# A fused attention and feed-forward kernel: the order of the first batch's loads and products

## The chip, the cores and the metric

The kernel runs on one core of one Trainium2 chip. The metric is the time of one execution on the device in microseconds (us). An execution with the hardware profiler on gives the span, from the first to the last instruction of the program, and the trace that the lines below come from.

## The reference

Attention without softmax over 8 batches of 12 heads, 448 positions and 64 values a head, then a gated feed-forward layer over the 3584 rows that come out:

```python
scores = (1.0 / np.sqrt(64)) * np.matmul(q, k.transpose(0, 1, 3, 2))
attn = np.maximum(scores, 0.0) ** 2 / 448
x = np.matmul(attn, v).transpose(0, 2, 1, 3).reshape(3584, 768)
gate = np.maximum(x @ w_gate, 0.0)      # w_gate, w_val: 768 x 1536
val = x @ w_val
out = (gate * val) @ w_out              # w_out: 1536 x 768
```

Inputs and output are float32. Products are made in bfloat16.

## The kernel before

**Loads.** GpSimd (POOL) issues all loads (`dma_in`, L246), and they turn float32 into bfloat16 on the way. They run on one queue in the order of the calls at the end of the kernel (L689 to L724), and POOL holds eight of them outstanding: each issue waits for the load eight places ahead of it. `load_heads(b, h0, n, what)` loads keys and queries (tile `qk`, two DMAs) or values (tile `vv`, two DMAs) of n heads. `load_gv(c)` loads 256 columns of `w_gate` and of `w_val` (tiles `wg`, `wv`, 384 KB each), `load_out(c)` half the columns of `w_out` (tiles `wo`).

**Attention.** Three groups g of four heads per batch. Batches 0 and 1 transpose `qk` on TensorE (PE) against an identity (`transpose_pair`, L346, tile `t_ps`) and copy the result to `qkT` (L355). Batches 2 to 7 are transposed by DMA: VectorE (DVE) gathers the rows into `spare` (seven copies, L377), then SyncE (SP) issues two DMA transposes (L387), which write `qkT`. A copy of one element, `mark` (L712), on POOL waits for them ahead of the next batch's loads. Scores come in steps `Part.s(i)`: the product (L469, and L475 for the last 64 keys, the tail), relu on ScalarE (ACT, L485) or DVE (L487), square on DVE (L503, tile `at` or `spare`). `Part.pv` multiplies by the values (L525, L531) and a copy (L547, L549) fills `xT`.

**Batch 0 in two parts.** Its queries are cut into a part A of 192 columns and a part B of 256, so that the feed-forward of part A can begin early. The order of batch 0's PE work is a string, `ORDER` (L754): `T2` is a transpose step of two heads, `A1:0` score step 0 of group 1 in part A, `VA1` that group's product with values, `W2` two products of 128x512 on zeros whose result is not used (`idle`, L334); an `f` has the step use two single banks of PSUM, and `/` begins a new burst. Eight products on zeros run ahead of all (`first_zeros`, L747).

**Feed-forward.** For each block of 128 columns mf, a gate product (`g_ps`) and a value product (`v_ps`), six matmuls each (L578), then relu (L585, L587) and the product of both on DVE (L592) into `hT`. Each waits for its `xT` and its weight block. In batch 0 the order over parts and blocks is made by `ffn_ops` (L606): part A with the first `n1` blocks, part B with the same, then both in turn. Output tiles follow: per 128 rows two products of 12 matmuls (L630, `o_ps`), copies on ACT (L643), and two stores of 64 rows on SP (L674). Over two batches there are seven such tiles.

**Order on the engines.** `plan` (L103) walks through the attention list, the feed-forward list, the loads and the rest with rough costs, and so fixes the order in which each engine's instructions stand. Between attention bursts of later batches it puts feed-forward work worth `gap`, which is the work left in the batch divided by the bursts left (L158 to L160). On the chip each engine takes its own instructions in that order.

Of the kernel before, what the change touches and what calls it, by code (L numbers as in the profile page):

```python
# [102 lines left out]
def plan(att, ffn, others, pool, nburst, calm):  # L103

    P = Planner()
    ai = fi = pi = 0
    pend = list(others)
    last_burst = None  # L110
    since = 0.0
    gap = 0.0
    while ai < len(att) or fi < len(ffn) or pend or pi < len(pool):
        cands = []
        for op in pend:
            b = P.best(op)
            if b is not None:
                cands.append((b[0], op.prio, b[2], 1, b[1], op))
        if pi < len(pool):
            b = P.best(pool[pi])  # L120
            if b is not None:
                s = b[0]
                if pi >= P.NOUT:
                    s = max(s, P.landed[pi - P.NOUT])
                cands.append((s, 0, 0.0, 0, "POOL", pool[pi]))
        A = P.best(att[ai][0]) if ai < len(att) else None
        F = P.best(ffn[fi][1]) if fi < len(ffn) else None
        pick = None
        if A is not None and F is not None:
            if att[ai][1] == last_burst:  # L130
                pick = "A" if A[0] <= F[0] + 0.3 else "F"
            elif since >= gap:
                pick = "A" if A[0] <= F[0] + 0.1 else "F"
            else:
                pick = "F" if F[0] <= A[0] + 0.1 else "A"
        elif A is not None:
            pick = "A"
        elif F is not None:
            pick = "F"
        if pick == "A":  # L140
            cands.append((A[0], 2, A[2], 2, "PE", att[ai][0]))
        elif pick == "F":
            cands.append((F[0], 2, F[2], 2, "PE", ffn[fi][1]))
        assert cands, "no operation can start"
        s, _, _, kind, e, op = min(cands, key=lambda c: c[:4])
        P.commit(op, s, e)
        if kind == 0:
            pi += 1
        elif kind == 1:
            pend.remove(op)  # L150
        elif pick == "A":
            if att[ai][1] != last_burst:
                last_burst = att[ai][1]
                since = 0.0
            ai += 1

            b0 = ffn[fi][0] if fi < len(ffn) else None
            work = sum(o.engs["PE"] for b, o in ffn[fi:fi + 60] if b == b0)  # L158
            left = nburst(b0, last_burst) if b0 is not None else 1
            gap = work / max(1, left) if left > 0 and last_burst >= calm else 0.0  # L160
        else:
            since += op.engs["PE"]
            fi += 1
    order = sorted(range(len(P.ops)), key=lambda i: (P.ops[i].start, i))
    return [P.ops[i] for i in order]
# [3 lines left out]
def kernel(  # L169
# [14 lines left out]
    B, H, S, D = q.shape  # L184
# [5 lines left out]
    NT = S // P2  # L190
    NC = NT // 2
# [5 lines left out]
    KF = d_ff // 128  # L197
# [47 lines left out]
    def dma_in(dst, src, n_desc, kb, deps=(), alloc=(), rate=380.0):  # L245
        op = Op({"POOL": 0.58 + 0.0004 * n_desc}, lambda: nc.gpsimd.dma_start(out=dst(), in_=src),  # L246
                deps=deps, alloc=alloc, xfer=kb / rate)
        op.lat = 0.75 if n_desc <= 128 else 1.3
        pool_ops.append(op)
        return op  # L250

    wg_op, wv_op, wo_op = {}, {}, {}

    def load_gv(c):
        cols = slice(c * WC, (c + 1) * WC)
        wg = moe_w_gate.rearrange("(kd p) f -> p kd f", p=128)
        wv = moe_w_val.rearrange("(kd p) f -> p kd f", p=128)
        wg_op[c] = dma_in(lambda: w_gate_sb[c], wg[:, :, cols], 768, 720)
        wv_op[c] = dma_in(lambda: w_val_sb[c], wv[:, :, cols], 768, 720)

    def load_out(c):
        wo = moe_w_out.rearrange("(kf p) m -> p kf m", p=128)
# [17 lines left out]
    def load_heads(b, h0, n, what="kv"):  # L280
        if b not in bat:
            bat[b] = Batch()
            bat[b].buf = Buf(r_in, NT if b >= XBAR_FROM else HP)
            bat[b].vbuf = Buf(r_v, NQ * len(PARTS(b)))
            bat[b].tbuf = Buf(r_xb, NQ * (2 * NC + 1) if b > 0 else NQ * (NC + 1) * len(PARTS(b)))
            bat[b].qk_op, bat[b].v_op = {}, {}
        st = bat[b]

        def tile_of(name, n):
            if not hasattr(st, name):  # L290
                setattr(st, name, inp.tile([128, H, n, D], BF16, name=name))
            return getattr(st, name)

        hs = slice(h0, h0 + n)
        rows = lambda x: x[b, hs].rearrange("h (p t) d -> p h t d", t=NT)
        rate = (240.0 if h0 == 4 else 290.0) if b == 0 else 340.0
        if "k" in what:
            k_op = dma_in(lambda: tile_of("qk", NT)[64:128, hs], rows(k), 64 * n, 112 * n, rate=rate, alloc=[st.buf] if h0 == 0 else [])
            q_op = dma_in(lambda: tile_of("qk", NT)[0:64, hs], rows(q), 64 * n, 112 * n, rate=rate)
            for h in range(h0, h0 + n):  # L300
                st.qk_op[h] = (k_op, q_op)
        if "v" in what:
            v0 = dma_in(lambda: tile_of("vv", NC + 2)[0:64, hs, 1:NC + 2], rows(v)[:, :, 0:NC + 1], 64 * n, 64 * n,
                        alloc=[st.vbuf] if h0 == 0 else [], rate=340.0)
            v1 = dma_in(lambda: tile_of("vv", NC + 2)[64:128, hs, 0:NC + 1], rows(v)[:, :, NC:NT], 64 * n, 64 * n, rate=340.0)
            for h in range(h0, h0 + n):
                st.v_op[h] = (v0, v1)

# [27 lines left out]
    def transpose_pair(b, g, j):  # L336

        st = bat[b]
        ps = Buf(r_f, 1)
        box = {}  # L340

        def emit():
            t_ps = box["t"] = bank("t_ps", BF16)
            for i, t in enumerate(slot_order(b)):
                for h2 in range(2):
                    nc.tensor.transpose(t_ps[64 * h2:64 * h2 + 64, i * 128:(i + 1) * 128],  # L346
                                        st.qk[:, 4 * g + 2 * j + h2, t, :], ident)

        def emit_copy():
            dst = columns_of(b)[:, :, 2 * g + j, :].rearrange("p a (t c) -> p t a c", c=P2)  # L350
            src = box["t"][:, :2 * S].rearrange("p (t a c) -> p t a c", t=NT, a=2)
            if cp.eng == "ACT":
                nc.scalar.copy(dst, src)
            else:
                nc.vector.tensor_copy(dst, src)  # L355

        h = 4 * g + 2 * j
        op = Op({"PE": 0.5 if g or b else 0.95}, emit, deps=list(st.qk_op[h]) + list(st.qk_op[h + 1]) + [id_op],
                alloc=[ps], reads=[st.buf])
        cp = Op({"DVE": 0.57, "ACT": 0.84}, emit_copy, deps=[op], alloc=[st.tbuf] if g == 0 and j == 0 else [],  # L360
                reads=[ps], prio=0, bias=0.0)
        others.append(cp)
        t_op[(b, 2 * g + j)] = cp
        return op
# [199 lines left out]
    def gv_ops(b, c0, n, mf):  # L564
# [28 lines left out]

        pe = {"PE": 0.03 + 6 * n / 2400.0}
        ga, va, gs = Buf(r_f, 1), Buf(r_f, 1), Buf(r_g, 1)
        gop = Op(pe, lambda: product("g_ps", w_gate_sb), deps=xop[(b, c0)] + [wg_op[c]], alloc=[ga], reads=[st.x_buf])
        grel = Op(on_psum(n), None, deps=[gop], alloc=[gs], reads=[ga], prio=0)
        grel.emit = lambda: emit_relu(grel)
        vop = Op(pe, lambda: product("v_ps", w_val_sb), deps=xop[(b, c0)] + [wv_op[c]], alloc=[va], reads=[st.x_buf])
        vmul = Op({"DVE": 0.09 + n / 960.0}, emit_mul, deps=[vop, grel], alloc=[hs["buf"]] if first else [],  # L600
                  reads=[va, gs], prio=0)
        hs["mul"].append(vmul)
# [3 lines left out]
    def ffn_ops(b):  # L606
        res = []
        if len(PARTS(b)) == 2:
            pa, pb = PARTS(b)
            n1 = KF // 2  # L610
            order = [(pa, m) for m in range(n1)] + [(pb, m) for m in range(n1)]
            order += [(p, m) for m in range(n1, KF) for p in (pa, pb)]
        else:
            order = [(PARTS(b)[0], m) for m in range(KF)]
# [76 lines left out]
    id_op = Op({"POOL": 0.35}, identity)  # L691
    pool_ops.append(id_op)
    load_heads(0, 4, 4, "k")
    load_heads(0, 0, 4, "v")
    load_heads(0, 8, 4, "k")
    load_heads(0, 4, 8, "v")
    load_gv(0)
    load_gv(1)
    load_gv(2)
    load_heads(1, 0, 4)  # L700
    load_gv(3)
    load_heads(1, 4, 4)
    load_gv(4)
    load_gv(5)
    load_out(0)
    load_heads(1, 8, 4)
# [40 lines left out]
    def first_zeros():  # L747
# [3 lines left out]
    att.append((Op({"PE": 3.0}, first_zeros), nb))  # L751


    ORDER = ("T0 W2 T1 A0:0f A0:1 W2 A0:3 W2 A0:2 T2 T3 A1:0 A1:1f A1:3 T4 T5 A1:2 A2:0 A2:1f A2:2 VA0f A2:3 "  # L754
             "B0:0 VA1f B0:3 VA2f B0:1f B0:2 / B1:0 B2:0 VB0f / / B2:1f / B1:2 B2:3 B1:3 B1:1 / / B2:2 VB1f VB2")
    for x in ORDER.split():
        part = {"A": A, "B": Bp}
        single = x[-1] == "f"
# [78 lines left out]
```

## Time and profile before

| | |
|---|---|
| runs | 437.32, 438.71, 438.66, 439.34 us; median 438.69 |
| profiled execution | 437.32 us, span 435.6 us |
| mean granted clock of TensorE | 0.995 |
| PE busy | 424.9 us (98%) in 3014 matmuls |
| DVE, ACT, POOL busy | 231.5, 198.6, 46.3 us |
| first products: gate and value (L578), outputs (L630) | 127.3, 127.0, 113.2 us |
| HBM read, written | 48.76 MB, 11.01 MB |

The engines run side by side; each waits for another only through semaphores. In a timeline row stand the start, the time taken (of several instructions in a row, marked x), the engine, the line, the operation with out<-in, the shape, and in brackets the idle time before it with what ended it. A `POOL` row of a load or an `SPq` row of a store is its issue; the data land later. PEclk is the share of TensorE's clock that was granted.

### The profile page before, as it was taken

What the parts mean: (1) busy time and instruction counts of PE and PEld (TensorE: products, weight loads), DVE (VectorE), ACT (ScalarE), POOL (GpSimd) and SP (SyncE); (2) the same over time, 40 slices, a digit from 0 to 9 for tenths busy, and PEclk for the clock granted to TensorE, in tenths of its full rate; (3) what the DMA queues carried; (4) which work ended last, traced back from release to release, by engine and by line L of the source; (5) the groups of instructions that cost most, each with busy time, mean ns of one, the idle gap of its engine ahead of it and who ended that gap; (6) DMA issues with size and microseconds to landing.
All of it is one profiled execution on the core that took longest, in us unless ns stands there. A gap on an engine that the chain in (4) does not pass through costs nothing.

```text
span 435.6 us, 7425 instructions
## 1 busy us (share of the span) xinstructions
PE 424.9 (98%) x3014; PEld 223.7 (51%) x3014; DVE 231.5 (53%) x411; ACT 198.6 (46%) x340; POOL 46.3 (11%) x72
## 2 busy tenths in 40 slices
PE   6799999999999999999999999999999999999996
PEld 2577875444454444544455444554445444555553
DVE  3796776177625775674653746545643456202200
ACT  3685455345634554554454545544544444332221
POOL 8546210010001002000200200010000000000000
PEclk9899999999999999999999999999999999999999
DMA  8999999980289567927937990980003200040014
GB/s 111 195 198 198 202 201 214 141 147 14 40 160 203 71 87 106 208 55 109 169 67 118 166 151 15 150 146 2 0 2 86 62 0 2 9 101 0 2 36 108
DMA packets 75170, 44.12 MB, mean 101 GB/s; under 512 B 34560, under 2 KB 71680, under 8 KB 75136
## 3 DMA queue, kind: packets, MB, share of 16 engines
q0 software_dynamic: 37856, 24.38, 39.7%
q1 hardware_dynamic: 37200, 19.17, 22.8%
q8 instruction: 23, 0.38, 0.3%
q10 hardware_dynamic: 80, 0.10, 0.1%
q14 instruction: 11, 0.09, 0.1%
HBM read 48.76 MB, written 11.01 MB: 137 GB/s over the span
## 4 chain that ended last, share of the span: by engine, by line
PE 93%; DMA 4%; POOL 1%; ACT 1%; SPq 0%; issue 0%; DVE 0%; POOLq 0%
PE o_ps L630 26%; PE g_ps L578 25%; PE v_ps L578 25%; PE s_ps L469 7%; PE s_ps L531 6%; DMA qkT<-spare 2%; DMA qk<-in_q_dram 2%; PE s_ps L475 2%; PE s_ps L525 1%; POOL qk L246 1%; PE t_ps L346 1%; PE x_ps L531 1%; ACT r_sb L485 0%; POOL vv L246 0%; SPq L387 0%
## 5 line engine op out<-in xcount | busy, mean ns | idle before, releaser
L578 PE MATMUL g_ps<-xT,wg 128*128 128x448 bf16 (+2 forms) x648 | 127.3, 332 | 0.1
L578 PE MATMUL v_ps<-xT,wv 128*128 128x448 bf16 (+2 forms) x648 | 127.0, 332 | 0.0
L485 ACT ACTIVATE r_sb<-s_ps 128x896 bf16<-128x896 f32 (+4 forms) x146 | 99.8, 739 | 36.0 <-PE s_ps L469 25.1
L592 DVE TENSOR_TENSOR hT<-v_ps,g_sb 128x448 bf16<-128x448 f32 (+2 forms) x108 | 61.5, 569 | 102.0 <-PE v_ps L578 101.9
L630 PE MATMUL o_ps<-wo,hT 128*128 128x384 bf16 x672 | 113.2, 326 | 0.0
L503 DVE TENSOR_TENSOR at<-r_sb 128x896 bf16<-128x896 bf16 (+4 forms) x163 | 93.6, 612 | 22.3 <-ACT r_sb L485 22.1
L585 ACT ACTIVATE g_sb<-g_ps 128x448 bf16<-128x448 f32 (+2 forms) x106 | 53.9, 508 | 110.5 <-PE g_ps L578 107.8
L630 PEld LDWEIGHTS <-hT 128*128 128x128 bf16 x672 | 63.9, 98 | 48.7 <-issue 8.0
L487 DVE TENSOR_SCALAR r_sb<-s_ps 128x448 bf16<-128x448 f32 (+5 forms) x72 | 62.5, 898 | 49.7 <-PE s_ps L469 49.5
L578 PEld LDWEIGHTS <-wv 128*128 128x128 bf16 x648 | 61.0, 98 | 50.7 <-issue 5.8
L578 PEld LDWEIGHTS <-wg 128*128 128x128 bf16 x648 | 59.8, 98 | 52.7 <-issue 10.4
L643 ACT ACTIVATE o_sb<-o_ps 128x384 f32<-128x384 f32 (+1 forms) x56 | 27.4, 489 | 71.6 <-PE o_ps L630 71.6
L469 PE MATMUL s_ps<-qkT 64*128 64x448 bf16 (+2 forms) x324 | 37.5, 336 | 1.8 <-DVE qkT L355 1.1
L531 PE MATMUL s_ps<-at,vv 128*64 128x448 bf16 x252 | 27.8, 357 | 0.0
L547 ACT CAST xT<-s_ps 128x896 bf16<-128x896 f32 (+1 forms) x22 | 19.6, 892 | 12.7 <-PE s_ps L531 12.7
L469 PEld LDWEIGHTS <-qkT 64*128 64x128 bf16 x324 | 11.8, 95 | 22.5 <-issue 15.5
L531 PEld LDWEIGHTS <-vv 128*64 128x64 bf16 x324 | 15.6, 109 | 14.1 <-issue 7.0
L246 POOL DMA_DIRECT2D vv<-in_v_dram x22 | 15.5, 717 | 46.4 <-PE s_ps L531 36.0
L712 POOL COPY mark<-qkT 64x1 bf16<-64x1 bf16 x5 | 0.9, 182 | 173.2 <-DMA qkT<-spare 173.2
L377 DVE COPY spare<-qk 128x768 bf16<-128x768 bf16 x42 | 12.3, 351 | 0.7 <-DMA qk<-in_q_dram 0.7
L355 DVE COPY qkT<-t_ps 128x896 bf16<-128x896 bf16 x12 | 7.1, 621 | 9.4 <-PE t_ps L346 9.3
L346 PE MATMUL t_ps<-ident,qk 128*64 128x128 bf16 x168 | 6.7, 235 | 3.3 <-DMA qk<-in_q_dram 2.6
(31 smaller groups left out, 83.6 us busy)
## 6 DMA issues: line engine op xcount, KB each, us to landing
out_dram<-o_sb SPq DMA_DIRECT2D x54, 192.0 KB, 2.8
vv<-in_v_dram POOLq DMA_DIRECT2D x12, 384.0 KB, 12.4
qk<-in_k_dram POOLq DMA_DIRECT2D x6, 672.0 KB, 7.3
qk<-in_q_dram POOLq DMA_DIRECT2D x6, 672.0 KB, 10.0
wg<-in_moe_w_gate_dram POOLq DMA_DIRECT2D x6, 384.0 KB, 11.2
wv<-in_moe_w_val_dram POOLq DMA_DIRECT2D x6, 384.0 KB, 11.9
wo<-in_moe_w_out_dram POOLq DMA_DIRECT2D x2, 1152.0 KB, 19.2
qk<-in_k_dram POOLq DMA_DIRECT2D x5, 224.0 KB, 10.1
```

The source lines that it names most:

```text
L246: op = Op({"POOL": 0.58 + 0.0004 * n_desc}, lambda: nc.gpsimd.dma_start(out=dst(), in_=src), deps=deps, alloc=alloc, xfer=kb / rate)
L469: nc.tensor.matmul(half_of(h2)[:, m * n:(m + 1) * n], lhsT=kq(1, j, h2, key_off(b) + c * 128, 128), rhs=kq(0, j, h2, self.c0, n), start=Tr ...
L485: nc.scalar.activation(dst, src, AF.Relu)
L487: nc.vector.tensor_scalar_max(dst, src, 0.0)
L503: lambda: nc.vector.tensor_tensor(self.at_tile(i), loc["r"][:, :2 * ne], loc["r"][:, :2 * ne], ALU.mult),
L531: nc.tensor.matmul(x_of(o, j), lhsT=st.vv[:, 4 * g + 2 * j + h2, 1 + c, :], rhs=self.at(j, c, h2), start=False, stop=(c == NC - 1))
L547: nc.scalar.copy(dst, src)
L578: nc.tensor.matmul(ps, lhsT=w[c][:, kd, o:o + 128], rhs=st.xT[:, kd, cols], start=(kd == 0), stop=(kd == KD - 1))
L585: nc.scalar.activation(loc["gs"], loc["g_ps"], AF.Relu)
L592: nc.vector.tensor_tensor(hs["hT"][:, mf, t0:t0 + n], loc["v_ps"], loc["gs"], ALU.mult)
L630: nc.tensor.matmul(loc["o"], lhsT=hs["hT"][:, kf, ti * 128:(ti + 1) * 128], rhs=w_out_sb[hf][:, kf, :], start=(kf == 0), stop=(kf == KF - 1))
L643: nc.scalar.activation(out=dst, in_=src, func=AF.Copy, scale=float(out_scale))
```

## The change

The loads of batch 0 take a new order: keys and queries of all heads first, then all values in two DMAs, then weights. The first 256 columns of both weights come in two steps of 128 columns. Weight blocks 3 and 4 each move one place forward against batch 1's heads. A weight block is waited for by its 128 columns (`wg_op[mf]`). Part A takes eight weight blocks before part B (`n1`). `ORDER` is new, with 19 products on zeros in it instead of 6. Copies of the first transposes of groups 1 and 2 in batch 0 go to ACT. In `plan`, 2.0 is taken from the work ahead of `gap`. Some rates in the planner's costs change. The stores are of 64 rows in both programs.

```diff
--- before.py
+++ after.py
@@ -155,9 +155,9 @@
             ai += 1
 
             b0 = ffn[fi][0] if fi < len(ffn) else None
-            work = sum(o.engs["PE"] for b, o in ffn[fi:fi + 60] if b == b0)
+            work = sum(o.engs["PE"] for b, o in ffn[fi:fi + 60] if b == b0) - 2.0
             left = nburst(b0, last_burst) if b0 is not None else 1
-            gap = work / max(1, left) if left > 0 and last_burst >= calm else 0.0
+            gap = max(0.0, work) / max(1, left) if left > 0 and last_burst >= calm else 0.0
         else:
             since += op.engs["PE"]
             fi += 1
@@ -251,12 +251,18 @@
 
     wg_op, wv_op, wo_op = {}, {}, {}
 
-    def load_gv(c):
-        cols = slice(c * WC, (c + 1) * WC)
+    def load_gv(c, parts=1):
         wg = moe_w_gate.rearrange("(kd p) f -> p kd f", p=128)
         wv = moe_w_val.rearrange("(kd p) f -> p kd f", p=128)
-        wg_op[c] = dma_in(lambda: w_gate_sb[c], wg[:, :, cols], 768, 720)
-        wv_op[c] = dma_in(lambda: w_val_sb[c], wv[:, :, cols], 768, 720)
+        n = WC // parts
+        for i in range(parts):
+            o = slice(i * n, (i + 1) * n)
+            cols = slice(c * WC + i * n, c * WC + (i + 1) * n)
+            kb, rate = 720 // parts, 380.0 if parts == 1 else 320.0
+            g = dma_in(lambda o=o: w_gate_sb[c][:, :, o], wg[:, :, cols], 768, kb, rate=rate)
+            v = dma_in(lambda o=o: w_val_sb[c][:, :, o], wv[:, :, cols], 768, kb, rate=rate)
+            for m in range(cols.start // 128, cols.stop // 128):
+                wg_op[m], wv_op[m] = g, v
 
     def load_out(c):
         wo = moe_w_out.rearrange("(kf p) m -> p kf m", p=128)
@@ -301,8 +307,8 @@
                 st.qk_op[h] = (k_op, q_op)
         if "v" in what:
             v0 = dma_in(lambda: tile_of("vv", NC + 2)[0:64, hs, 1:NC + 2], rows(v)[:, :, 0:NC + 1], 64 * n, 64 * n,
-                        alloc=[st.vbuf] if h0 == 0 else [], rate=340.0)
-            v1 = dma_in(lambda: tile_of("vv", NC + 2)[64:128, hs, 0:NC + 1], rows(v)[:, :, NC:NT], 64 * n, 64 * n, rate=340.0)
+                        alloc=[st.vbuf] if h0 == 0 else [], rate=340.0 if b else 380.0)
+            v1 = dma_in(lambda: tile_of("vv", NC + 2)[64:128, hs, 0:NC + 1], rows(v)[:, :, NC:NT], 64 * n, 64 * n, rate=340.0 if b else 380.0)
             for h in range(h0, h0 + n):
                 st.v_op[h] = (v0, v1)
 
@@ -357,7 +363,7 @@
         h = 4 * g + 2 * j
         op = Op({"PE": 0.5 if g or b else 0.95}, emit, deps=list(st.qk_op[h]) + list(st.qk_op[h + 1]) + [id_op],
                 alloc=[ps], reads=[st.buf])
-        cp = Op({"DVE": 0.57, "ACT": 0.84}, emit_copy, deps=[op], alloc=[st.tbuf] if g == 0 and j == 0 else [],
+        cp = Op({"ACT": 0.84} if b == 0 and g and j == 0 else {"DVE": 0.57, "ACT": 0.84}, emit_copy, deps=[op], alloc=[st.tbuf] if g == 0 and j == 0 else [],
                 reads=[ps], prio=0, bias=0.0)
         others.append(cp)
         t_op[(b, 2 * g + j)] = cp
@@ -593,10 +599,10 @@
 
         pe = {"PE": 0.03 + 6 * n / 2400.0}
         ga, va, gs = Buf(r_f, 1), Buf(r_f, 1), Buf(r_g, 1)
-        gop = Op(pe, lambda: product("g_ps", w_gate_sb), deps=xop[(b, c0)] + [wg_op[c]], alloc=[ga], reads=[st.x_buf])
+        gop = Op(pe, lambda: product("g_ps", w_gate_sb), deps=xop[(b, c0)] + [wg_op[mf]], alloc=[ga], reads=[st.x_buf])
         grel = Op(on_psum(n), None, deps=[gop], alloc=[gs], reads=[ga], prio=0)
         grel.emit = lambda: emit_relu(grel)
-        vop = Op(pe, lambda: product("v_ps", w_val_sb), deps=xop[(b, c0)] + [wv_op[c]], alloc=[va], reads=[st.x_buf])
+        vop = Op(pe, lambda: product("v_ps", w_val_sb), deps=xop[(b, c0)] + [wv_op[mf]], alloc=[va], reads=[st.x_buf])
         vmul = Op({"DVE": 0.09 + n / 960.0}, emit_mul, deps=[vop, grel], alloc=[hs["buf"]] if first else [],
                   reads=[va, gs], prio=0)
         hs["mul"].append(vmul)
@@ -607,7 +613,7 @@
         res = []
         if len(PARTS(b)) == 2:
             pa, pb = PARTS(b)
-            n1 = KF // 2
+            n1 = 2 * KF // 3
             order = [(pa, m) for m in range(n1)] + [(pb, m) for m in range(n1)]
             order += [(p, m) for m in range(n1, KF) for p in (pa, pb)]
         else:
@@ -691,16 +697,15 @@
     id_op = Op({"POOL": 0.35}, identity)
     pool_ops.append(id_op)
     load_heads(0, 4, 4, "k")
-    load_heads(0, 0, 4, "v")
     load_heads(0, 8, 4, "k")
-    load_heads(0, 4, 8, "v")
-    load_gv(0)
+    load_heads(0, 0, H, "v")
+    load_gv(0, 2)
     load_gv(1)
     load_gv(2)
+    load_gv(3)
     load_heads(1, 0, 4)
-    load_gv(3)
+    load_gv(4)
     load_heads(1, 4, 4)
-    load_gv(4)
     load_gv(5)
     load_out(0)
     load_heads(1, 8, 4)
@@ -751,8 +756,8 @@
     att.append((Op({"PE": 3.0}, first_zeros), nb))
 
 
-    ORDER = ("T0 W2 T1 A0:0f A0:1 W2 A0:3 W2 A0:2 T2 T3 A1:0 A1:1f A1:3 T4 T5 A1:2 A2:0 A2:1f A2:2 VA0f A2:3 "
-             "B0:0 VA1f B0:3 VA2f B0:1f B0:2 / B1:0 B2:0 VB0f / / B2:1f / B1:2 B2:3 B1:3 B1:1 / / B2:2 VB1f VB2")
+    ORDER = ("W1 T0 W2 T1 W2 A0:0f A0:1 W3 A0:2 W4 T2 T3 W2 A1:0 A0:3 W2 A1:1 A1:3 T4 T5 W2 A2:0f A2:2 A1:2 A2:1f W1 A2:3 / "
+             "B0:0 VA0f VA1f VA2 B0:1f B0:3 B0:2 / B2:0 B1:0 B1:3 VB0f / B1:1 B2:1f / / / B2:2 B1:2 VB1f B2:3 VB2")
     for x in ORDER.split():
         part = {"A": A, "B": Bp}
         single = x[-1] == "f"
```

## Prediction

> **What bounds the kernel now.** I read the page first, then the stretch table, TensorE's timeline, and the timelines of the two queues that issue DMAs. The page says TensorE and little else:
>
> ```profile
> PE 424.9 (98%) x3014; PEld 223.7 (51%) x3014; DVE 231.5 (53%) x411; ACT 198.6 (46%) x340; POOL 46.3 (11%) x72
> ...
> PEclk9899999999999999999999999999999999999999
> ```
>
> Of the 435.6 us, 10.7 are idle on PE, nearly all before 20 us or behind the last product, and the clock digit drops once. The stretch table says where (columns: stretch, length, busy time of PE, PEld, DVE, ACT, POOL, granted clock, DMA share, GB/s):
>
> ```profile
> 14.50:18.00 3.50, 3.11 (x44) 2.35 (x44) 2.33 (x6) 1.36 (x3) 1.95 (x4) 0.51 1.46 198
> 18.00:20.00 2.00, 1.64 (x32) 0.98 (x28) 2.00 (x5) 2.00 (x6) 0.64 (x2) 1.00 1.45 197
> 20.00:30.00 10.00, 10.00 (x142) 7.35 (x142) 9.54 (x20) 8.66 (x18) 3.08 (x5) 1.00 1.42 199
> ```
>
> So only the first 20 us have PE time to win; yet the loads run at 198 GB/s without a break through all of it. The deciding view sets PE's timeline against POOL's. POOL keeps eight loads outstanding: each issue waits for the load eight places earlier and starts 0.28 us after that has landed. So POOL's rows are a list of landings:
>
> ```profile
> 17.59 0.62 POOL L246 DMA_DIRECT2D qk<-in_q_dram  x1 [0.77 <-DMA vv<-in_v_dram]
> ...
> 23.52 0.83 POOL L246 DMA_DIRECT2D wg<-in_moe_w_gate_dram  x1 [1.38 <-DMA wg<-in_moe_w_gate_dram]
> 25.59 0.83 POOL L246 DMA_DIRECT2D wv<-in_moe_w_val_dram  x1 [1.23 <-DMA wv<-in_moe_w_val_dram]
> ...
> 30.07 0.62 POOL L246 DMA_DIRECT2D qk<-in_q_dram  x1 [1.33 <-DMA wv<-in_moe_w_val_dram]
> ```
>
> The last values landed at 17.31, the second pair of weight blocks at 23.24 and 25.31, the third `wv` at 29.79. PE starts the product that needs the second `wv` here:
>
> ```profile
> 25.35 0.67 PE L578 MATMUL v_ps<-xT,wv 128*128 128x192 bf16 x6
> ```
>
> That is 0.04 us after the landing: a load, not TensorE, set the time at 25.35. What PE lost before, the half clock included, was hidden behind weights that were not there yet. From 25.35 PE is full to its last product, but for 0.13 us at 81 us and one wait, where batch 2's DMA transposes arrive just too late:
>
> ```profile
> 88.98 0.74 PE L469 MATMUL s_ps<-qkT 64*128 64x448 bf16 x6 [0.18 <-DMA qkT<-spare]
> ```
>
> ```profile
> 73.05 0.38 PE L475 MATMUL s_ps<-qkT 64*64 64x448 bf16 x4
> ...
> 74.81 4.07 PE L630 MATMUL o_ps<-wo,hT 128*128 128x384 bf16 x24
> 78.81 0.38 PE L525 MATMUL s_ps<-at,vv 64*64 64x448 bf16 x4
> ...
> 80.38 1.60 PE L578 MATMUL g_ps<-xT,wg 128*128 128x448 bf16 x6
> ```
>
> ```profile
> 68.99 5.79 SPq L674 DMA_DIRECT2D out_dram<-o_sb  x4
> 74.89 9.81 SPq L387 DMA_TRANSPOSE qkT<-spare  x2
> ```
>
> SP is in order: the transposes stand behind the four stores of the first two output tiles.
>
> **Part by part.** The profiled execution is the base: 435.6 us of span and 1.72 around it, 437.32, the fastest of four runs whose median is 438.69.
>
> *Keys and queries first.* Heads 8 to 11 no longer stand behind 0.5 MB of values: their q landed at 14.63 (POOL's row at 14.91) and the two loads in front took 1.43 us (10.96 to 12.39), so they land at 13.2. The bytes up to the last value are the same, so that stays at 17.3 and now holds every product with values. TensorE can do scores earlier but reaches weights no earlier: worth nothing unless the weights are on time.
>
> *Thirteen more products on zeros* (27 for 14), at 0.21 us each (eight in 3.39 were at half clock, two later in about 0.54) 2.8 us. They, and the transposed copies moved to ACT (0.89 us for a 128x896 cast beside 0.62 on DVE, so a pair runs side by side instead of 1.16 in a row), lie ahead of the weights. Cover: after the values PE's queue holds 14.9 us of work up to the wait priced next (three value products of 0.82, 13 weight products of 0.50, six score steps of 0.33, three more at 0.9 together, two value products of 1.03, tails and 0.1 per change of array shape). It starts at some 18.0 (values at 17.3, and the last squares of the first part are due then), so it ends at 32.9, about 1 us before the weights. Without that cover zeros put in late would cost up to 2.8.
>
> *Eight weight steps on the first part instead of six* (`n1`), loads 3 before batch 1, and the first pair in halves. In the changed queue PE meets the value product of the fourth `wv` before any product of part two. It has by then done, beyond what it had done at 25.35: eight products of 192 columns (0.50, 4.0), two value products (25.95 to 26.98 and 32.03 to 33.04, 2.04), four score steps (0.33, 1.3), two tails (0.24, 0.48), four more changes of shape (24.03 less 23.43 is 0.60 instead of 0.50; 0.4). Sum 8.2. The kernel breaks even here if that `wv` lands at 25.35 + 8.2 = 33.55. It lands at 17.31 plus six whole loads and four halves. Whole loads took 1.96 to 2.08 on average over neighbouring landings; I take 2.0. A half has as many packets with half the bytes. By bytes it takes 0.99. By packets: the trace's load packets last 60 ns at 512 B, 79 at 768 and 88 at 896, a line that gives 41 at 256; at the measured overlap of 1.42, 48 per engine make 1.39. I take 1.2, between the two because transfers of 896 B packets run at nearly the same GB/s as those of 512 B. So 17.31 + 12.0 + 4.8 = 34.1: **+0.55**, bounds 33.0 (-0.55, where PE's own pace takes over) and 35.35 (+1.8).
>
> A rule speaks against the halves: the Trainium skill, DMA: Bandwidth & Descriptors, Specifications, wants at least 512 B per transfer for line rate, with read-modify-write below. Its section "Why small descriptors are slow" gives 3 cycles on top of 8 for 256 B, an estimate of 1.15 us a half, and the sum would be 0.2 lower. No load of before has such packets.
>
> POOL issues four halves for two wholes (0.83 each) and two value loads fewer (0.65): 0.4 us more on a queue that issues some eight loads ahead. Batch 1's loads follow 4 loads later in queue order, needed 2.6 us after the fourth `wv`, landed 2.0 to 2.3 after: nothing, but thin.
>
> *The planner's gap less 2.0.* It moves attention steps forward. The program's order shows one place where that counts. Before: output tile, scores, tile, tail and values, tile, values, seven products, batch 2's scores. After: scores, tile, tail and values, tile, values, tile, values, seven products, batch 2's scores. So the second tile, whose stores stand ahead of the transposes on SP, ends nearer to those scores: before 88.80 - 73.05 = 15.75 us, after 1.57 (values, 78.81 to 80.38) + 4.00 (tile, 74.81 to 78.81) + 8.42 (products to 88.80) = 13.99. Transposes were issued 1.84 after the tile's end (74.89 - 73.05) and the copies ahead of them end no later. From issue to use the five batches with a marker row took 14.09, 13.73, 12.34, 12.25 and 13.02:
>
> ```profile
> 88.98 0.18 POOL L712 COPY mark<-qkT 64x1 bf16<-64x1 bf16 x1 [30.69 <-DMA qkT<-spare]
> 129.27 0.18 POOL L712 COPY mark<-qkT 64x1 bf16<-64x1 bf16 x1 [38.30 <-DMA qkT<-spare]
> ```
>
> The wait becomes 1.84 + 13.09 - 13.99 = 0.94 at their mean, 0.1 to 1.94 at the ends; 0.18 was there. **+0.75** (-0.1 to +1.75). PE, DVE and ACT behind it are in order, and nothing is idle later to give it back. Later batches have 5 us or more between landing and use.
>
> *Stores per 64 rows*: both programs store 64x768; nothing changes, no cost.
>
> Sum +1.3: span 436.9, time **438.6**, which is the median of before to 0.02%.
>
> **Rivals.** *The halves cost as much as wholes* (slower). If time goes by packets without more overlap, each takes up to 2.0 us; the fourth `wv` lands at 37.3, +3.8, with the transposes 441.9. It decides from 1.55 us per half (fourth `wv` at 35.5, time 440.0). For it: no 256 B load is in the trace; against: packets of 512 to 896 B moved 198 to 229 GB/s, nearly the same, where a price per packet would have parted them by 1.75.
>
> *Before is usually worse than its profile* (faster). Three of its runs took 1.3 to 2.0 us longer. The half clock lasted 3.4 us from 14.55 and fell where PE waited for loads anyway; between 18 and 25 it would cost up to half its length, 1.7. With the weights by bytes (33.3, -0.25), and the transposes in 12.25, the changed kernel takes 437.0, 0.4% under the median, and with more products ahead it may lose the dip. The Trainium skill, TensorE: Matmul & The Clock Gate, "What's actually happening", says that the window of 3.4 us runs free, so that its place differs by run; one trace can't show that.
>
> *The clock gained is gained time* (the change as it looks): 1.6 us from 14.5 to 18 would come off. The row at 25.35 speaks against it: PE would wait there.
>
> **How the numbers follow.** A measurement of this kernel tells 0.3% (1.3 us) from no change. Forecast within it: 0.45. Faster, nearly all by the second rival: 0.27. Slower, by the halves or by transposes of 14 us and more on top of late weights: 0.28. The range goes from the faster case, 437.0, past both terms at their upper ends (435.6 + 1.8 + 1.75 + 1.72 = 440.9) to most of the slower rival, 441.2.
>
> **What would show it.** Right: no clock dip before 18 us; a `v_ps` product with an idle of 0.3 us or more ended by `wv` near 34; batch 2's first scores with an idle of 0.5 to 1.5 ended by `qkT<-spare`, SP's transposes at 76 to 78. Wrong: half loads landing over 1.55 apart, PE idle between 20 and 30, or no wait at 34 and none at 90.

## The result and the profile after

The changed kernel takes 439.36 us (median of 53 runs, 437.81 to 442.84). The kernel before, run beside it, takes 438.37 us (79 runs, 437.09 to 440.15). The ratio is 1.0022, 95% interval 1.0015 to 1.0030: about 1 us slower. The forecast was 438.6 against a median of 438.69, so no change; its range holds the time. The profiled execution took 439.10 us with a span of 437.4, where that of before took 437.32 and 435.6.

The page after, engine busy times and clock digits:

```profile
PE 427.9 (98%) x3027; PEld 224.0 (51%) x3027; DVE 226.7 (52%) x404; ACT 201.7 (46%) x346; POOL 46.8 (11%) x72
...
PEclk9999999999999999999999999999999999999999
```

The dip of the clock is gone, thirteen more matmuls ran, and the span is 1.8 us longer. So here the clock gained was not time gained. The rows that carry the loss are in TensorE's timeline:

```profile
33.66 0.67 PE L584 MATMUL v_ps<-xT,wv 128*128 128x192 bf16 x6 [0.78 <-DMA wv<-in_moe_w_val_dram]
...
36.65 0.97 PE L352 MATMUL t_ps<-ident,qk 128*64 128x128 bf16 x28 [0.32 <-DMA qk<-in_q_dram]
...
65.21 1.03 PE L475 MATMUL s_ps<-qkT 64*128 64x448 bf16 x6
...
90.71 0.74 PE L475 MATMUL s_ps<-qkT 64*128 64x448 bf16 x6 [1.18 <-DMA qkT<-spare]
```

PE waits at 33.66 for the fourth `wv`, at 36.65 for batch 1's queries, and 1.18 us at 90.71 for batch 2's DMA transposes, where before it waited 0.18. At 65.21 a score step has only one value product between it and the score step before (63.78), and takes 1.03 instead of the usual 0.74. SP's queue shows why the transposes are late (start, time, operation):

```profile
70.81 6.87 SPq L680 DMA_DIRECT2D out_dram<-o_sb  x4
77.79 10.72 SPq L393 DMA_TRANSPOSE qkT<-spare  x2
88.56 1.57 SPq L680 DMA_DIRECT2D out_dram<-o_sb  x2
```

The two stores of the second output tile end at 77.67 and the transposes are issued at 77.79, 2.9 us later than before (74.89), though the rows that they read had been copied by 74.21. POOL's rows that wait for a DMA are again landings, 0.28 us ahead of each start. They show the last values, the last two of the four half loads (`wg`, `wv`) and the fourth `wv`:

```profile
17.73 0.82 POOL L246 DMA_DIRECT2D wv<-in_moe_w_val_dram  x1 [2.10 <-DMA vv<-in_v_dram]
...
20.51 0.63 POOL L246 DMA_DIRECT2D qk<-in_k_dram  x1 [0.24 <-DMA wg<-in_moe_w_gate_dram]
21.60 0.62 POOL L246 DMA_DIRECT2D qk<-in_q_dram  x1 [0.46 <-DMA wv<-in_moe_w_val_dram]
...
33.90 0.62 POOL L246 DMA_DIRECT2D qk<-in_q_dram  x1 [1.63 <-DMA wv<-in_moe_w_val_dram]
```

The last values landed at 17.45, the four halves at 18.09, 19.16, 20.23 and 21.32 (3.87 us for four, 0.97 each; the first two by the landing times in the trace, since POOL was still issuing then), the fourth `wv` at 33.61.

### The profile page after: what moved, and what is told of

It is laid out like the page before. It is cut to its first block, busy times and chain, and to the rows that moved or that the text cites. A ratio compares the mean times of both kernels' runs of the same rounds, so it can differ in the third digit from the quotient of the medians.

```text
span 437.4 us, 7430 instructions
## 1 busy us (share of the span) xinstructions
PE 427.9 (98%) x3027; PEld 224.0 (51%) x3027; DVE 226.7 (52%) x404; ACT 201.7 (46%) x346; POOL 46.8 (11%) x72
## 4 chain that ended last, share of the span: by engine, by line
PE 89%; DMA 8%; POOL 2%; issue 0%; SPq 0%; DVE 0%; ACT 0%; POOLq 0%
PE o_ps L636 26%; PE v_ps L584 24%; PE g_ps L584 24%; PE s_ps L475 7%; PE s_ps L537 6%; DMA qk<-in_q_dram 3%; DMA wv<-in_moe_w_val_dram 2%; DMA qkT<-spare 2%; PE s_ps L481 2%; POOL qk L246 1%; PE s_ps L531 1%; PE t_ps L352 1%; POOL wg L246 0%; POOL vv L246 0%; SPq L393 0%
## 5 line engine op out<-in xcount | busy, mean ns | idle before, releaser
L491 ACT ACTIVATE r_sb<-s_ps 128x448 bf16<-128x448 f32 (+5 forms) x151 | 102.6, 734 | 27.4 <-PE s_ps L475 21.8
L509 DVE TENSOR_TENSOR at<-r_sb 128x896 bf16<-128x896 bf16 (+3 forms) x163 | 93.8, 611 | 28.5 <-ACT r_sb L491 28.3
L493 DVE TENSOR_SCALAR r_sb<-s_ps 128x896 bf16<-128x896 f32 (+4 forms) x67 | 59.1, 907 | 42.2 <-PE s_ps L475 41.6
L553 ACT CAST xT<-s_ps 128x896 bf16<-128x896 f32 (+2 forms) x23 | 20.1, 874 | 13.8 <-PE s_ps L537 13.8
L537 PEld LDWEIGHTS <-vv 128*64 128x64 bf16 x324 | 15.6, 109 | 14.1 <-issue 7.2
L246 POOL DMA_DIRECT2D vv<-in_v_dram x20 | 14.3, 725 | 43.8 <-PE s_ps L537 33.1
L340 PE MATMUL w_ps<-zeros 128*128 128x512 bf16 x27 | 9.1, 457 | 1.4 <-DVE zeros L753 1.3
L361 DVE COPY qkT<-t_ps 128x896 bf16<-128x896 bf16 x10 | 6.0, 621 | 8.4 <-PE t_ps L352 8.4
```

The lines of the kernel that those rows point to most:

```text
L491: nc.scalar.activation(dst, src, AF.Relu)
L493: nc.vector.tensor_scalar_max(dst, src, 0.0)
L509: lambda: nc.vector.tensor_tensor(self.at_tile(i), loc["r"][:, :2 * ne], loc["r"][:, :2 * ne], ALU.mult),
L537: nc.tensor.matmul(x_of(o, j), lhsT=st.vv[:, 4 * g + 2 * j + h2, 1 + c, :], rhs=self.at(j, c, h2), start=False, stop=(c == NC - 1))
```

## The experiments

The theory: batch 2's transposes behind the second tile's stores on SP cost the 1 us, the first 35 us net out. The rivals: the loss comes from the first part (weights, zeros, load order), or there is none beyond the spread of load landings from run to run.

**The same two programs again.** Two more profiles of each, unaltered.

> The kernel before, unchanged, profiled again. Theory (the landing of a weight block sets the span): span = landing of the second wv + 410.2 to 410.4, or later if a later wv is waited for; a span of 436 to 437.5 goes with a landing of 25.7 to 27. Rival (the place of the half clock sets it): the landing stays at 25.3 and a longer span comes with the clock lowered between 18 and 25.

> As the other look at the kernel before: span = landing of the second wv + 410.3 (0.3 either way) by the theory; by the rival it goes with the place of the half clock.

> The changed kernel, unchanged, profiled again. Theory: span = landing of the fourth wv + 402.0 + the wait of batch 2's scores (0.5 to 1.9, from transposes issued 1.7 us after the second tile's end) + the wait of batch 1's first transposes (0 to 0.4). Rival: wait at batch 2's scores only by chance in the first profile, here under 0.3.

> As the other look at the changed kernel: landing of the fourth wv + 402.0 + the waits at batch 1's first transposes and batch 2's scores, the last 0.5 to 1.9 by the theory, under 0.3 by the rival.

They took 439.26 and 437.96 us (before), 439.82 and 439.72 us (after). TensorE's timeline of the longer run of before, and its stretch table (columns as in the first one shown):

```profile
27.47 0.67 PE L578 MATMUL v_ps<-xT,wv 128*128 128x192 bf16 x6 [0.91 <-DMA wv<-in_moe_w_val_dram]
```

```profile
14.50:18.00 3.50, 2.19 (x34) 1.78 (x34) 2.27 (x5) 0.65 (x3) 1.64 (x2) 0.50 1.44 197
18.00:20.00 2.00, 1.88 (x22) 1.11 (x22) 1.34 (x4) 2.00 (x4) 0.69 (x2) 0.50 1.46 196
20.00:24.00 4.00, 4.00 (x73) 2.79 (x70) 3.59 (x8) 4.00 (x11) 1.47 (x3) 1.00 1.46 197
```

Here the half clock lasted 6.83 us, from 13.19 to 20.02, and still PE was early: it stood 0.91 us before the second `wv`, which landed at 27.43, because the last values had landed at 19.66 instead of 17.31. In the other run of before they landed at 17.71 and the clock was at half for 3.4 us. So in these three profiles of before the span goes with the landing of the loads. Span less landing of the last values:

| | last values landed | span | difference |
|---|---|---|---|
| before, three profiles | 17.31, 19.66, 17.71 | 435.6, 437.6, 436.2 | 418.3, 417.9, 418.5 |
| after, four profiles (the fourth is timed below) | 17.45, 18.61, 19.19, 18.54 | 437.4, 438.1, 438.0, 438.1 | 420.0, 419.5, 418.8, 419.6 |

The means are 418.2 and 419.5. This difference, 1.2 us, is close to that of the medians, 0.99. In before the spans lie 2.0 us apart and the differences 0.6, so the landings carry most of that spread. In after the differences (1.2) lie further apart than the spans (0.7). There the fourth `wv` does better: its landing (33.61, 35.19, 35.47, 35.43) plus 402.0, plus the waits and the long score step behind it, gives 437.4, 438.1, 438.2 and 438.0 against 437.4, 438.1, 438.0 and 438.1. The 402.0 is taken from the runs below that have no later wait.

The landings are not the whole account of before's long runs. For 99 runs of before, timed beside the experiments below, the mean granted clock is known. In 25 of them it is under 0.989, and these took 439.73 us at the median; the other 74 took 437.78. No trace of such a run was kept, so whether the low clock makes a run long or comes of loads that are late is not shown. The longest half clock that a trace shows is the 6.83 us above, where the loads set the time.

The two runs of after shown here, whose values came later, wait for the transposes too, by less:

```profile
91.46 0.74 PE L475 MATMUL s_ps<-qkT 64*128 64x448 bf16 x6 [0.86 <-DMA qkT<-spare]
```

```profile
91.36 0.74 PE L475 MATMUL s_ps<-qkT 64*128 64x448 bf16 x6 [0.48 <-DMA qkT<-spare]
```

**The planner's gap undone.**

```diff
-            work = sum(o.engs["PE"] for b, o in ffn[fi:fi + 60] if b == b0) - 2.0
+            work = sum(o.engs["PE"] for b, o in ffn[fi:fi + 60] if b == b0)
```

> The changed kernel with the planner's 2.0 taken out again, so the output tiles stand in the order of before. Theory (the loss is batch 2's transposes behind the second tile's stores): SP issues them near 74.7, batch 2's first scores wait 0 to 0.3 instead of 1.18, and the back-to-back score steps near 65 are gone (0.3): 438.1 to 438.4, ratio to before 0.999 to 1.000. Rival (the extra products on zeros, or the half loads, cost the time): stays at 439.2 to 439.5, ratio 1.002.

438.66 us beside 438.07, ratio 1.0014 (0.9997 to 1.0031). The transposes are issued at 76.34 and land at 90.23, 0.05 us before batch 2's first scores start; their row has no wait. The fourth `wv` came late (34.83), and PE waited 1.32 us for it:

```profile
34.88 0.67 PE L584 MATMUL v_ps<-xT,wv 128*128 128x192 bf16 x6 [1.32 <-DMA wv<-in_moe_w_val_dram]
```

```profile
90.28 0.74 PE L475 MATMUL s_ps<-qkT 64*128 64x448 bf16 x6
```

The wait at 90 goes with the edit. Whether the time does is not told by this interval.

**The second tile's stores on ACT's queue.** In the changed kernel, for batch 0 and `ti == 1` alone:

```diff
-                    others.append(Op({"SP": 0.2}, lambda f=emit_store: f(0, d_model, both), deps=cps, reads=[obuf],
-                                     xfer=1.5))
+                    others.append(Op({"ACT" if aq else "SP": 0.2}, lambda f=emit_store, qs=[(0, nc.scalar), (1, nc.scalar)] if aq else both: f(0, d_model, qs),
+                                     deps=cps, reads=[obuf], xfer=1.5))
```

> The changed kernel with the two stores of batch 0's second output tile issued by ACT instead of SP; the order of TensorE stays. Theory: SP's transposes are issued when the copies end, near 74.3, the scores wait for nothing: 1.1 to 1.2 less than the changed kernel, 438.2, ratio to before 0.999 to 1.000. Rival (the transposes are late because their data are late or the DMA engines are full): the wait at 90 stays over 0.8 and the ratio at 1.002.

438.05 us beside 438.07, ratio 0.9999 (0.9982 to 1.0016). SP's queue now:

```profile
70.56 1.19 SPq L680 DMA_DIRECT2D out_dram<-o_sb  x2
74.49 12.40 SPq L393 DMA_TRANSPOSE qkT<-spare  x2
```

Two stores are gone from it, the transposes are issued at 74.49, and the only wait after 20 us that is left is 0.70 for the fourth `wv` at 33.92. Span 435.9 with values at 17.21.

**Both once more on one chip, and a dose.** The third of these cuts the same two stores into four of 32 rows, on SP:

```diff
-                        queue.dma_start(out=dst, in_=src)
+                        if b == 0 and ti == 1:
+                            for r in range(0, 64, 32):
+                                queue.dma_start(out=dst[r:r + 32], in_=src[r:r + 32])
+                        else:
+                            queue.dma_start(out=dst, in_=src)
```

> The changed kernel, unaltered, timed beside the next two on one chip. Theory (a steady loss at batch 2's transposes, about 1 us): 1.0 to 1.4 us above the next run, whose only edit is the queue of two stores. Rival (the two already overlap and the earlier distance was chance): within 0.5 us of it.

> The changed kernel with the two stores of batch 0's second output tile issued by ACT instead of SP, unaltered from the earlier run of this edit. Theory: no idle of PE at 90 us, and a median within 0.5 us of before. Rival: as slow as the changed kernel.

> The changed kernel with the two stores of batch 0's second output tile cut into four of 32 rows, all still on SP: a dose of the suspected cost, same bytes, same engines otherwise. An issue of a store took 0.55 us on SP, so the transposes are issued 1.1 us later. Theory: the wait at batch 2's scores grows by 1.1 to about 2.2 us, and the time with it, to 440.2 to 440.6 us against 439.4 for the changed kernel. Rival (the wait is absorbed later, or the transposes' own transfers and not their issue set the landing): no more than 0.3 us above the changed kernel.

Measured, 12 runs each: 439.40 us unaltered, 438.34 with the stores on ACT (in its profile batch 2's first scores start at 89.97 without a wait), 439.65 with four stores; before beside them 438.27. The first two differ by 1.06 us, and by 0.36 to 1.42 in 95 of 100 resamplings of the two sets of runs. SP's queue with four stores:

```profile
77.48 1.75 SPq L682 DMA_DIRECT2D out_dram<-o_sb  x4
79.35 10.42 SPq L393 DMA_TRANSPOSE qkT<-spare  x2
```

Batch 2's first scores, unaltered and then with four stores:

```profile
91.41 0.74 PE L475 MATMUL s_ps<-qkT 64*128 64x448 bf16 x6 [0.58 <-DMA qkT<-spare]
```

```profile
91.47 0.74 PE L475 MATMUL s_ps<-qkT 64*128 64x448 bf16 x6 [1.02 <-DMA qkT<-spare]
```

So taking the stores off SP gives back the loss, all of it within the intervals: 439.40 to 438.34, where before is 438.27. The dose was smaller than forecast: four stores of 32 rows took 1.75 us to issue where two of 64 take 1.1 to 1.2, not twice that. The wait grew from 0.58 to 1.02, the median by 0.25, which 12 runs do not tell from nothing. So the time falls when the wait is taken away; that it follows the wait one to one is shown neither way (the waits were 0.48 to 1.18 us in four profiles).

**The gap alone, in the kernel before** (the edit of the first experiment, the other way).

> The kernel before with the planner's 2.0 alone. In its order the second tile ends later against the transposes, but one more product stands before batch 2's scores. Theory: transposes issued near 77, scores wait (issue + 13 against 15.1 after the tile's end) 0 to 0.8: ratio 1.000 to 1.002. Rival (the loss is in the first 40 us): ratio 1.000, no wait at 90 over 0.2.

438.08 us, ratio 1.0005 (0.9986 to 1.0024). The transposes are late here too, but batch 2's scores start at 90.51, behind eight products after the third tile where the changed kernel has seven, and do not wait:

```profile
70.71 6.87 SPq L674 DMA_DIRECT2D out_dram<-o_sb  x4
77.70 10.50 SPq L387 DMA_TRANSPOSE qkT<-spare  x2
```

So the gap makes the transposes late, but the wait comes only with the order that the planner makes of the whole change, with one product less there.

**Zeros added to the kernel before**: `W2` behind `T3`, `W3` behind `A1:3` in its `ORDER`.

> The kernel before with five more products on zeros, W2 after T3 and W3 after A1:3, in the gaps ahead of the half clock; nothing else. Theory (the second wv sets 25.35 whatever PE does before): no dip of the clock, span within 0.3 of before, ratio 0.9995 to 1.0005. Rival (before's other runs are longer because of the half clock): 0.5 to 1.3 faster, ratio 0.997 to 0.999.

438.26 us, ratio 1.0004 (0.9987 to 1.0021). The dip of the clock is gone (1.000 in the profile, 0.995 or more in all 12 runs), and PE waits for the second `wv` instead:

```profile
26.04 0.67 PE L578 MATMUL v_ps<-xT,wv 128*128 128x192 bf16 x6 [0.55 <-DMA wv<-in_moe_w_val_dram]
```

The median did not fall, and three of the 12 runs still took over 439 us. This speaks against the clock as the cause of before's long runs, but the interval reaches down to 0.6 us faster, so it does not exclude it.

**Three parts of the changed kernel undone**, each in the version with the stores on ACT, so that the transposes don't hide it. The products on zeros out of `ORDER`:

```diff
-    ORDER = ("W1 T0 W2 T1 W2 A0:0f A0:1 W3 A0:2 W4 T2 T3 W2 A1:0 A0:3 W2 A1:1 A1:3 T4 T5 W2 A2:0f A2:2 A1:2 A2:1f W1 A2:3 / "
+    ORDER = ("T0 T1 A0:0f A0:1 A0:2 T2 T3 A1:0 A0:3 A1:1 A1:3 T4 T5 A2:0f A2:2 A1:2 A2:1f A2:3 / "
```

> The kernel of the run with stores on ACT, with all 19 products on zeros taken out of ORDER (the first eight stay). Theory (they lie where PE waits for weights): the clock dips once or twice before 25 us, PE idles more there, the wait for the fourth wv at 33.6 to 34.8 shrinks or stays, ratio to before 0.999 to 1.001. Rival (zeros keep a clock that is worth time): 0.5 to 1.5 us slower, ratio 1.001 to 1.003.

440.37 us beside 438.06, ratio 1.0039 (1.0021 to 1.0056): slower. The theory fell here: the zeros are not free filling. TensorE's timeline shows the same kind of product, 12 of 128x192, twice:

```profile
22.62 1.17 PE L537 MATMUL x_ps<-at,vv 128*64 128x192 bf16 x12
...
24.03 0.69 PE L537 MATMUL s_ps<-spare,vv 128*64 128x192 bf16 x12
```

Until 24 us all products run at this slower pace (the first transposes of 28 take 1.70 us, in the changed kernel 0.97). PE then comes to the fourth `wv` at 36.69, 2.06 us after it landed (34.63), and the span is 438.6 with values at 17.68, a difference of 420.9 where the version with zeros had 418.7 and 418.9. Ten of these 12 runs list a granted clock of 0.979 to 0.987; with the zeros in, all 24 runs (two times 12) have 0.998 or more.

`load_gv(0)` whole, instead of `load_gv(0, 2)`:

> The kernel of the run with stores on ACT, with the first weights loaded whole again. Theory (a half load costs by its bytes, 1.0 us): the fourth wv lands 0 to 0.3 earlier or at the same time, ratio to before 0.999 to 1.000. Rival (halves cost up to 1.4 each): it lands 1.6 earlier, and the time falls by 0.7 or more, as far as PE's own pace allows.

438.31 us, ratio 0.9999 (0.9983 to 1.0014); fourth `wv` at 33.67, PE's wait 0.45. Values of heads 0 to 3 ahead of the keys and queries of heads 8 to 11:

> The kernel of the run with stores on ACT, with the values of heads 0 to 3 loaded ahead of the keys and queries of heads 8 to 11 again, as before. Theory (keys first brings scores earlier but no weights): the last values and the fourth wv land at the same time, PE idles 0.3 more near 15, ratio to before 0.999 to 1.001, the same as with keys first. Rival (keys first is worth the 1.4 us by which those heads land earlier): 0.5 to 1.4 us slower than the run with stores on ACT.

438.48 us, ratio 1.0004 (0.9988 to 1.0020); fourth `wv` at 34.45, wait 0.92. Neither edit is worth anything that can be measured.

**A version meant to be better**: the gap undone, part B's score step 3 of group 2 ahead of `VB1f` in `ORDER`, and the planner's rate for batch 1's first keys and queries at 220.

> A version meant to beat both: the changed kernel without the planner's 2.0, with B2:3 ahead of VB1f in ORDER, and with the planner told that batch 1's first keys and queries arrive later (220 instead of 340), so that TensorE has 1.5 us more to do before it meets the fourth wv and batch 1's first transposes. Theory: idle near 34 falls from 0.7 to 1.3 to under 0.4, no wait at 36 and none over 0.3 at 90: 437.3 to 437.8, ratio to before 0.997 to 0.9995. Rival (the loads' landing moves everything behind it whatever the order): ratio 1.000 to 1.001 as with the 2.0 undone.

438.20 us, ratio 0.9997 (0.9981 to 1.0013). The wait for `wv` fell to 0.15, and batch 1's first transposes took its place:

```profile
37.80 0.97 PE L352 MATMUL t_ps<-ident,qk 128*64 128x128 bf16 x28 [1.10 <-DMA qk<-in_q_dram]
```

No version here beats the kernel before by more than its interval.

## Why the prediction was wrong where it was

**The step that failed: "which is the median of before".** The sum was +1.3 on a profiled execution of 437.32. That execution was the fastest of four, and only six of before's 79 runs lie under it. The prediction then set the 438.6 against the median of before, 438.69, and so forecast no change, although its own sum made the changed kernel 1.3 us slower than the execution that it started from. For the 1.4 us between that execution and the median it had only its second rival, the half clock that the change might remove. The half clock is gone (granted clock 0.995 or more in all 54 runs of after for which it is known), and the changed kernel is still 0.99 us slower. The execution that the sum started from was one of early loads: its last values landed at 17.31, against 17.71 and 19.66 in the two other profiles of before and 17.45 to 19.19 after. Of the 1.06 us between the difference forecast (438.62 less 438.69) and the one measured (+0.99), 0.48 is the sum (438.62 against 439.10 in the profile), 0.26 the changed kernel's median above that profile, and 0.32 the median of before, 438.37 on 79 runs instead of 438.69 on four. A difference between two programs belongs on the median as well as on the profile: +1.3 on 438.37 would have been 439.7; measured 439.36. How much of before's spread is its clock stays open.

**Weights: +0.55 forecast, about +0.1 in the profile.** The break-even was worked out as 33.55 and the fourth `wv` forecast at 34.1. In the three profiles of the changed order with no later wait (two with the stores on ACT, one with the gap undone) the span is that landing plus 402.0 (33.88 to 435.9, 34.83 to 436.9, 34.63 to 436.6), and before's 435.6 is reached at 33.6: the break-even held. The landing was 33.61 in this profile. From the last values it came 16.16 later, in the three other runs of after 16.58, 16.28 and 16.88, against 16.8 forecast: in this profile the four halves were 0.9 faster than taken, and over the four runs the six whole loads 0.2 to 1.0 slower than 12.0 (12.29 in this profile, 13.01 in the run of after timed last). For a half the prediction stood between 0.99 by bytes and 1.39 by packets. Its packet time was right (the 256-byte packets lasted 41 ns at the median), but not the overlap of 1.42 that it kept: between 17.45 and 21.32 the DMA share was 1.70, against 1.43 while the wholes came (23.36 to 33.61). PE's queue was to end at 32.9 and ended at 33.66 − 0.78 = 32.88.

**Transposes: +0.75 forecast, +1.0 measured** (1.18 less 0.18), in the place and by the queue named; 0.94 of wait was the forecast. Of its three numbers, 1.84 us from the tile's end to the issue came out as taken, issue to use was 12.92 for 13.09, and the scores would have started 13.58 after the tile's end, not 13.99; the last two errors partly cancel. In the later runs the wait was 0.48 to 0.86, as issue to landing fell to 12.2 to 12.6 us.

**Two terms were missing**: 0.32 at batch 1's first transposes ("nothing, but thin") and 0.29 at 65.21, where two score steps stand only one product apart. With 0.1 and 1.0 they make 1.7 of the span's 1.8. One reading was loose, though nothing in the sum rests on it: the loads do not run at 198 GB/s through all of the first 20 us (67 and 147 in the first two stretches of 5 us).

**Zeros: no net cost, right, for half the reason.** They lie ahead of the weights as forecast. But leaving them out costs 2.0 to 2.3 us (440.37 against 438.05 and 438.34, with before at 438.06 to 438.27 beside them), where the prediction had them worth nothing: in the new order the full pace of the first 24 us comes with them. **Keys and queries first** and the halves: worth nothing, as forecast.

**The rivals.** *Halves as wholes* fell: 0.97 us each, decisive only from 1.55. *Before is usually worse than its profile* was right that its median lies above its profile, and its long runs do list a lower clock; that the clock is the cause is not shown, and losing the dip did not make the changed kernel faster. *The clock gained is gained time* fell for the profiled runs with the rows of 27.47 and 26.04, and with the result.

The Trainium skill, DMA: Bandwidth & Descriptors, Specifications, wants 512 B per transfer for line rate; the halves, half as long in each run of bytes, landed at the pace of their bytes (0.97 us where wholes take about 2), so no penalty is to be seen here.

## What to carry to other kernels

Put a difference worked out from one profile on the median of the runs as well as on that profile, and ask of each cause of spread whether the changed program has it too. Before a spread is blamed on the clock or on the loads, read the landings in two or three profiles and the granted clock of all runs, and keep a profile of a long run. When a plan changes the order of work, look at what stands in front of the next transfers on an in-order queue: two stores that wait for their copies delayed transposes whose data lay ready 3.6 us earlier.

## What the runs showed of the hardware

- Without the 19 products on zeros the first 24 us ran at the slow pace (1.17 against 0.69 us for the same 12 matmuls), with PE 58% to 76% busy in the stretches 10 to 14.5, 14.5 to 18 and 18 to 20 us, and no idle over 1.78. The granted-clock column shows 1.00 for these stretches, since the trace has no record of the clock before 24.05: there the durations say more than the column. The Trainium skill, TensorE: Matmul & The Clock Gate, "What's actually happening", has the full clock come after some 3.4 us of sustained activity; here PE's last idle of size ends at 20.04, and full pace comes at 24.05, 4.0 us later.
- A half-clock stretch of 6.83 us in one run of before, twice as long as the 3.4 us of the two others, did not lengthen what follows, as PE waited 0.91 us for a load after it (27.47).
- Two DMA transposes of batch 2 took 13.4 to 14.1 us from first issue to last landing when issued by 77.00 (nine profiles; a tenth, without the zeros, took 15.5), and 12.1 to 12.9 when issued from 77.70 on (seven profiles). What sets it is open.
